# Two transformer layer pairs on one core: the first weight casts before the first turned rows' casts, and the norms' powers before GpSimd's masks

## The chip, the cores and the metric

The kernel runs on one core of one Trainium2 chip. The metric is device microseconds (us) of one execution; a measurement is the median of several runs. Engine names: PE is TensorE (matmuls and transposes), DVE is VectorE, ACT is ScalarE, POOL is GpSimd, SP is SyncE, which here only issues DMAs.

## The reference

Two layers are each applied twice to x of 2048 rows by 640 columns: attention with a window of 256, 32 heads of 20, then a block with a squared ReLU.

```
x = x + A(layernorm(x), wqkv, wo)          # causal, 256 keys back, softmax, times wo
x = x + B(layernorm(x), w1, b1, w2, b2)    # h = relu(x @ w1 + b1) ** 2;  h @ w2 + b2
x = x + A(layernorm(x), wqkv, wo)
x = x + B(layernorm(x), w1, b1, w2, b2)
```

## The kernel before, in words

The rows are cut into 8 groups of 256; with two layers that makes 16 units u. A unit's work is: layer norm; q, k and v (`stage_qk`, `stage_v`); scores, row maxima, exponentials and the product with v, four heads at a time (`max_quad`, `exp_quad`, `pv_quad`); the product with wo (`stage_o`); a second layer norm turned into columns (`stage_y`); and the block B (`stage_f`). Attention of one unit is interleaved with the dense products of the unit before it.

Each large product is done in f16 with both operands split into a high and a low half: three matmuls (high by high, high by low, low by high) stand for one. So each weight piece that arrives in f32 is cast on ACT (high half) and subtracted on DVE (low half): `convert`, lines 270 to 274. Activations that are turned by TensorE get the same pair, a cast on ACT (line 390) and a subtraction on DVE (line 391): `split_t`. The mean and variance of a layer norm come from DVE (lines 366 to 371), the power -0.5 from GpSimd (line 377, a [128,1] op), and DVE then scales the row tile (line 379).

The order on each engine is written out by a planner in the kernel: every piece of work but PE's is posted as a job with an engine, a cost, its dependencies and a priority (`post`). As the planned time passes, `pump` puts the first job of the list that is ready, and a list entry of lower `prio` number stands ahead. The costs and landing times are estimates (`LAND` 1800 ns, `WLAND` 4500 ns after the planned transfer); they decide the order alone. On the chip each engine runs its list in order and waits where an operand is late.

At the start, `ln_load(0, prio=0)` loads the first two row tiles of x and `load_wq` loads wqkv in pieces of 256 or 128 columns, converted 128 columns at a time; `ln_t(0)` turns the first two normed tiles. The masks that GpSimd writes into the exponentials are line 856 (four per four heads; DVE writes two more, line 865).

Of the kernel before, what the change touches and what calls it, by code (L numbers as in the profile page):

```python
# [14 lines left out]
ALU = mybir.AluOpType  # L15

P = 128
# [10 lines left out]
KC = D // P  # L28
# [17 lines left out]
def kernel(ctx: ExitStack, tc: tile.TileContext, x, wqkv, wo, w1, b1, w2, b2, out):  # L46
# [70 lines left out]
    LOOK, LAT, LAND, CROSS, WLAND = 250.0, 50.0, 1800.0, 3600.0, 4500.0  # L117
# [27 lines left out]
    def post(eng, cost, fn, *deps, wait=0.0, prio=1, **kw):  # L145

        j = Job(eng, cost, fn, [d for d in deps if d is not None], now[0] + wait, prio, **kw)
        k = len(pend)
        while k and pend[k - 1].prio > prio:
            k -= 1  # L150
        pend.insert(k, j)
        return j
# [5 lines left out]
    def dma(fn, size, *deps, n=1, cost=450.0, prio=1, **kw):  # L158

        return post("S", n * cost, fn, *deps, prio=prio, size=size, **kw)  # L160
# [109 lines left out]
    def convert(st, hi, low, n, load, *deps, prio=2):  # L270

        a = post("A", 20 + 0.9 * n, lambda: nc.scalar.activation(hi, st, AF.Copy, scale=WS), load, *deps, prio=prio)
        return post("D", 30 + 1.04 * n, lambda: nc.vector.scalar_tensor_tensor(low, st, WS, hi, op0=ALU.mult,
                                                                               op1=ALU.subtract), a, prio=prio)
# [3 lines left out]
    def load_wq():  # L278
        at = 0
        for lo, n in [(j * D + c, min(2 * P, D - c)) for c in (0, 2 * P, 4 * P) for j in range(2)] + [  # L280
                (2 * D + c, min(2 * P, D - c)) for c in (0, 2 * P, 4 * P)]:
            raw, o = (w1raw, at) if at + KC * n <= FC * D else (krow[2], at - FC * D)
            at += KC * n
            st = raw[:, o:o + KC * n].rearrange("p (c n) -> p c n", c=KC)
            load = dma(lambda st=st, lo=lo, n=n:
                       nc.sync.dma_start(st, wqkv[:, lo:lo + n].rearrange("(c p) n -> p c n", p=P)),
                       P * KC * n * 4, prio=0, land=WLAND)
            for z in range(0, n, P):
                c = slice(lo + z, lo + z + P)
                wqj[(lo + z) // P] = convert(st[:, :, z:z + P], wq_s[:, 0, :, c], wq_s[:, 1, :, c], KC * P, load,  # L290
                                             prio=1)

    rowset = {}

# [64 lines left out]
    def layernorm(src, y, *deps, prio=2):  # L359

        box = {}

        def stats(i):
            if i == 0:
                box["st"] = sb.tile([P, 2, 6], F32, name="bst", bufs=2)
            nc.vector.bn_stats(box["st"][:, i, :], src[:, i * HD:(i + 1) * HD])

        def var():
            box["mv"] = mv = sb.tile([P, 4], F32, name="bmv", bufs=2)
            nc.vector.bn_aggr(mv[:, 0:2], box["st"])  # L370
            nc.vector.tensor_scalar(mv[:, 2:3], mv[:, 1:2], 1e-5, YS ** -2, op0=ALU.add, op1=ALU.mult)

        j = None
        for i in range(2):
            j = post("D", 455, lambda i=i: stats(i), j, *(deps[i:i + 1] or deps), prio=prio)
        j = post("D", 400, var, j, prio=prio)
        j = post("G", 520, lambda: nc.gpsimd.tensor_tensor(box["mv"][:, 3:4], box["mv"][:, 2:3], neghalf,
                                                                   op=ALU.pow), j, prio=prio)
        j = post("D", 576, lambda: nc.vector.tensor_scalar(y, src, box["mv"][:, 0:1], box["mv"][:, 3:4],
                                                           op0=ALU.subtract, op1=ALU.mult), j, prio=prio)  # L380
        return j
# [43 lines left out]
    def ln_load(u, *deps, prio=2):  # L425

        l, g = divmod(u, NG)
        ys = []
        for i in range(2):
            xt = sb.tile([P, D], F32, name="xt", tag="xt", bufs=2)  # L430
            load = dma(lambda xt=xt, i=i: nc.sync.dma_start(xt, xsrc(l, 2 * g + i)), P * D * 4, *deps, prio=min(prio, 1))
            ys.append((xt, layernorm(xt, xt, load, prio=prio)))
        lns[u] = ys
# [608 lines left out]
    def stage_o(u):  # L1042
        if u not in ols:
            yield Want(opened, bank=False)
        od, x1b, js, xj = ols.pop(u)
        for i in range(2):
            x1, adds = x1b[i], []
            yield Want(*js[2 * i:2 * i + 2])
            need(*js[2 * i:2 * i + 2])
            for h in range(2):  # L1050
                yield Want()
                acc, jobs = mm_tile([P, 2 * T], "acc")
                hs = slice(h * HD, (h + 1) * HD)
                need(*woj.values())
                def add(x1=x1, acc=acc, hs=hs):
                    nc.vector.scalar_tensor_tensor(x1[:, hs], acc[:, :HD], 1.0 / (OS * WS), x1[:, hs],
                                                   op0=ALU.mult, op1=ALU.add)

                yield from mm3(acc[:, :HD], lambda a, k: od[:, k, a, i * P:(i + 1) * P],
                               lambda c, k: wo_s[:, c, k, hs], KC, 136,  # L1060
                               lambda wait: jobs.append(post("D", 408, add, xj[i], wait=wait, prio=0)))
                adds.append(jobs[0])
            y = sb.tile([P, D], F32, name="xt", tag="xt", bufs=2)
            x1s[u, i], ys[u, i] = x1, (y, layernorm(x1, y, *adds, prio=urgency["ln"]))
# [267 lines left out]
    spin(14)  # L1332
    ln_load(0, prio=0)
    load_wq()
    run(ln_t(0))
    spin(7)
# [91 lines left out]
```

## Time and profile before

| what | value |
|---|---|
| median of 3 runs | 1554.59 us (1553.53 to 1555.71) |
| the profiled execution's own time | 1555.59 us |
| its span in the trace | 1553.9 us |
| PE busy | 1530.8 us, 99% of the span |
| DVE / ACT / POOL busy | 67% / 43% / 29% |

The span runs from the first to the last record of the trace; the time has another 1.7 us around it. The profiled execution took 1.0 us more than the median. All stretches below are counted in us from the span's start. A row of the timeline gives start, duration (from the first start to the last end where several are merged), engine, line and operation, the tile written and the tile read, how many, and in brackets the idle time before it and what ended that.

### The profile page before, as it was taken

To read this page: it belongs to the slowest core of one execution; us is meant where nothing else is said; L and a number is where in the kernel's file an instruction comes from. 1 tells how busy PE (TensorE), PEld (TensorE's weight loads), DVE (VectorE), ACT (ScalarE), POOL (GpSimd) and SP (SyncE) were. 2 spreads that over 40 slices of the span, in tenths; PEclk is the share of its full clock that TensorE was granted. 3 is DMA by queue.
4 is the path that set the end of the run, shared out by engine and by line. 5 is a ranking of instruction groups with operands and counts; after the bars stand their busy time and mean duration, and the time that the engine had idled before them with its cause. 6 is when DMAs were issued, how large, how long until landed. Compare 5 with 4: busy or idle time off the path is not lost.

```text
span 1553.9 us, 58533 instructions
## 1 busy us (share of the span) xinstructions
PE 1530.8 (99%) x25832; PEld 1197.5 (77%) x25832; DVE 1036.8 (67%) x2246; ACT 670.0 (43%) x1367; POOL 453.0 (29%) x847
## 2 busy tenths in 40 slices
PE   8998999999999999999999999999999999999999
PEld 7766778787787877778777787877878777786777
DVE  8788775666766567665656767667665676767641
ACT  4564445344443534534343443444435345354422
POOL 1223314133231322314132241332314224142321
PEclk9999999999999999999999999999999999999999
DMA  9773353442534334343353434435343352432010
GB/s 283 206 224 100 78 130 86 117 101 80 127 69 125 86 105 114 61 128 79 110 130 65 122 82 130 89 81 128 67 131 79 104 121 62 121 86 64 27 62 18
DMA packets 240343, 162.34 MB, mean 104 GB/s; under 512 B 93016, under 2 KB 224088, under 8 KB 240088
## 3 DMA queue, kind: packets, MB, share of 16 engines
q1 hardware_dynamic: 234136, 149.09, 38.0%
q10 hardware_dynamic: 5952, 9.50, 2.1%
q8 instruction: 203, 3.33, 0.9%
q14 instruction: 52, 0.43, 0.1%
HBM read 79.76 MB, written 58.72 MB: 89 GB/s over the span
## 4 chain that ended last, share of the span: by engine, by line
PE 94%; DVE 3%; ACT 1%; issue 1%; POOL 0%; ACTq 0%; DVEq 0%; POOLq 0%
PE acc L340 74%; PE pv L933 8%; PE bb L705 5%; PE bb L842 5%; PE bb L933 2%; ACT pt L827 1%; DVE mx L722 1%; DVE bb L685 0%; PE bb L737 0%; PE bb L888 0%; DVE bb L719 0%; DVE qd L538 0%; POOL pt L856 0%; PE tr L404 0%; DVE mx L685 0%
## 5 line engine op out<-in xcount | busy, mean ns | idle before, releaser
L827 ACT ACTIVATE pt<-bb 128x640 f32<-128x640 f32 (+2 forms) x512 | 312.5, 683 | 164.7 <-PE bb L842 141.0
L856 POOL TENSOR_SCALAR_AFFINE_SELECT pt<-pt 64x256 f32<-64x256 f32 x448 | 198.5, 443 | 595.9 <-ACT pt L827 566.7
L340 PE MATMUL acc<-y,w_s 128*128 128x256 f16 x2880 | 330.3, 273 | 2.3 <-DVE y L391 2.1
L340 PE MATMUL acc<-w_s,hh 128*128 128x320 f16 (+1 forms) x2340 | 326.7, 297 | 0.1
L340 PEld LDWEIGHTS <-w_s 128*128 128x128 f16 x2880 | 276.2, 98 | 42.1 <-issue 3.2
L340 PEld LDWEIGHTS <-hh 128*128 128x128 f16 x2340 | 222.1, 98 | 86.8 <-issue 0.4
L722 DVE TENSOR_REDUCE mx<-bb 128x4 f32<-128x1024 f32 x224 | 273.1, 1223 | 6.7
L340 PE MATMUL acc<-yT,wq_s 128*128 128x256 f16 x2250 | 259.0, 273 | 2.4 <-DVE mT L797 0.7
L340 PEld LDWEIGHTS <-wq_s 128*128 128x128 f16 x2400 | 229.6, 98 | 36.5 <-issue 3.4
L865 DVE COPY_PREDICATED_SCALAR pt<-drop,zero 128x256 f32 x224 | 99.8, 498 | 138.9 <-ACT pt L827 138.6
L1121 POOL TENSOR_TENSOR r<-r 128x256 f32<-128x256 f32 x192 | 122.6, 659 | 214.6 <-ACT r L1117 212.0
L945 ACT COPY ot<-pv 128x256 f32<-128x256 f32 x128 | 47.7, 372 | 287.5 <-PE bb L933 255.3
L933 PE MATMUL pv<-pt,vt 64*32 64x128 f32 (+5 forms) x3840 | 168.1, 303 | 0.9 <-ACT vt L624 0.9
L1127 DVE TENSOR_TENSOR hh<-r,hh 128x256 f16<-128x256 f32 x192 | 90.5, 484 | 108.7 <-ACT hh L1124 104.3
L933 PE MATMUL bb<-pt,vt 64*32 64x192 f32 (+3 forms) x3584 | 154.6, 302 | 0.4 <-POOL pt L856 0.4
L719 DVE COPY_PREDICATED bb<-maskq,bb 128x256 f32<-128x256 uint16 x224 | 94.0, 424 | 84.8 <-PE bb L705 84.1
L933 PEld LDWEIGHTS pv<-pt,vt 64*32 64x32 f32 (+1 forms) x3840 | 126.1, 106 | 31.5 <-issue 3.3
L340 PE MATMUL acc<-wo_s,od 128*128 128x320 f16 x960 | 139.6, 300 | 2.1 <-ACT od L1024 2.0
L340 PE MATMUL acc<-wq_s,yT 128*128 128x320 f16 x900 | 130.4, 299 | 1.6 <-DVE kt L391 0.5
L1117 ACT ACTIVATE r<-acc,b1s 128x256 f32<-128x256 f32 x192 | 81.2, 477 | 95.3 <-PE acc L340 93.4
L340 PEld LDWEIGHTS <-od 128*128 128x128 f16 x960 | 91.1, 98 | 40.4 <-ACT od L1024 2.3
L933 PEld LDWEIGHTS bb<-pt,vt 64*32 64x32 f32 x3584 | 116.3, 106 | 1.6 <-POOL pt L856 0.9
(105 smaller groups left out, 1444.8 us busy)
## 6 DMA issues: line engine op xcount, KB each, us to landing
o<-ot SPq DMA_DIRECT2D x64, 256.0 KB
qt<-qk SPq DMA_DIRECT2D x30, 480.0 KB
kt<-qk SPq DMA_DIRECT2D x30, 480.0 KB
qk<-qd SPq DMA_DIRECT2D x15, 640.0 KB
od<-o SPq DMA_DIRECT2D x14, 640.0 KB
qk<-yl SPq DMA_DIRECT2D x13, 640.0 KB
xt<-in_A_x_dram SPq DMA_DIRECT2D x16, 320.0 KB
x<-in_A_x_dram SPq DMA_DIRECT2D x16, 320.0 KB
```

The costliest lines, as they stand in the source:

```text
L340: nc.tensor.matmul(acc, lhs(a, c), rhs(b, c), start=(k == 0), stop=(k == 3 * nk - 1))
L705: nc.tensor.matmul(flat[e][rows, o:o + b - a], qt[r, p, i * P + 64 * h:i * P + 64 * (h + 1)], kt[r, p, a + to:b + to], start=True, stop=Tr ...
L719: nc.vector.copy_predicated(wins[:, :, 4 * Q:], later, wins[:, :, :Q])
L722: nc.vector.tensor_reduce(most, wins[:, :, Q:], axis=mybir.AxisListType.X, op=ALU.max)
L827: return lambda: nc.scalar.activation(room_of(box)[:, a:b], bank[:, a:b], AF.Exp, scale=SCALE / (QS * QS))
L842: nc.tensor.matmul(flat[e][h * Q:(h + 1) * Q, c0:c1], kt[r, 2 * qd + j, k0:k0 + Q], qt[r, 2 * qd + j, q:q + c1 - c0], start=True, stop=Tru ...
L856: nc.gpsimd.affine_select(out=m, in_=m, pattern=[[0, 4], [-1 if k else 1, Q]], base=0, fill=0.0, compare_op=ALU.is_gt if k else ALU.is_ge, ...
L865: nc.vector.copy_predicated(m, drop[:, k:k + 1, :].bitcast(mybir.dt.uint16).to_broadcast([P, 4, Q]), zero.unsqueeze(1).to_broadcast([P, 4, ...
L933: nc.tensor.matmul(pv[h][32 * jj:32 * (jj + 1), q0 * Q:(q0 + w) * Q], vf[r, c:c + 32], boxes[e]["pt"][r, a:b], start=(k == 0), stop=(k == ...
L1117: nc.scalar.activation(box["r"], acc[:, f, :], AF.Relu, bias=b1s[:, f0 + f:f0 + f + 1], scale=1.0 / (YS * WS))
L1121: nc.gpsimd.tensor_tensor(box["r"], box["r"], box["r"], op=ALU.mult)
L1127: nc.vector.tensor_sub(hh[:, 1, f, :], box["r"], hh[:, 0, f, :])
```

## The change

Three arguments change. The planner is told that the first piece of wqkv lands sooner (`LAND` in place of `WLAND`); the cast and the subtraction of that piece's first 128 columns get priority 0 in place of 1; and the power of every layer norm gets priority 0 in place of the norm's own.

```
-                       P * KC * n * 4, prio=0, land=WLAND)
+                       P * KC * n * 4, prio=0, land=WLAND if at > KC * 2 * P else LAND)
...
                 wqj[(lo + z) // P] = convert(st[:, :, z:z + P], wq_s[:, 0, :, c], wq_s[:, 1, :, c], KC * P, load,
-                                             prio=1)
+                                             prio=0 if lo + z < P else 1)
...
         j = post("G", 520, lambda: nc.gpsimd.tensor_tensor(box["mv"][:, 3:4], box["mv"][:, 2:3], neghalf,
-                                                                   op=ALU.pow), j, prio=prio)
+                                                                   op=ALU.pow), j, prio=0)
```

What the planner makes of it. On ACT, at the start of the program (the first two rows below are the branch into the kernel and the load of the activation table; wq_s are the converted weights, w_s the place where the raw piece lands, yT the turned rows, bb the PSUM banks that hold the transposes):

```order
 L1423 UNCONDITIONAL_BRANCH
-L390 ACT_TABLE_LOAD
+L272 ACT_TABLE_LOAD
+L272 ACTIVATE wq_s<-w_s 128x5x128 x2
 L390 CAST yT<-bb_143 128x3x128
 L390 CAST yT<-bb_143 128x2x128
 L390 CAST yT<-bb_144 128x3x128
 L390 CAST yT<-bb_144 128x2x128
-L272 ACTIVATE wq_s<-w_s 128x5x128 x6
+L272 ACTIVATE wq_s<-w_s 128x5x128 x3
```

Both casts of the first piece (256 columns, two casts) moved from behind the four casts of the turned rows to ahead of them. On DVE one subtraction of the piece (line 273) moved the same way, ahead of the four of line 391; the second stays behind them.

On GpSimd, at the second layer norm of unit 0 (`stage_y`, around 130 us): pt holds the exponentials, bmv the statistics of a norm.

```order
 L377 TENSOR_TENSOR bmv<-bmv,neghalf 128x1
-L856 AFFINE_SELECT pt<-pt 64x4x64 x4
-L377 TENSOR_TENSOR bmv<-bmv,neghalf 128x1
+L856 AFFINE_SELECT pt<-pt 64x4x64
+L377 TENSOR_TENSOR bmv<-bmv,neghalf 128x1
+L856 AFFINE_SELECT pt<-pt 64x4x64 x3
 L1073 TENSOR_TENSOR x_1540<-x_1540,b2s 128x320 x2
```

The power of the second row tile moved ahead of three of the four masks. On DVE at the same place (line 379 scales that row tile, line 391 is the low half of the turned y, lines 719 and 722 find the row maxima in the banks, line 948 adds up the attention's output):

```order
 L273 SCALAR_TENSOR_TENSOR w_s<-kt_97,w_s 128x640
+L379 TENSOR_SCALAR xt<-x_1541,bmv 128x640
 L865 COPY_PREDICATED pt<-drop,zero 128x4x64 x2
 L719 COPY_PREDICATED bb_143<-maskq,bb_143 128x4x64
 L273 SCALAR_TENSOR_TENSOR w_s<-kt_97,w_s 128x640
-L379 TENSOR_SCALAR xt<-x_1541,bmv 128x640
-L722 TENSOR_REDUCE mx<-bb_143 128x4
 L391 TENSOR_TENSOR y_2056<-tr,y_2056 128x3x128
 L391 TENSOR_TENSOR y_2056<-tr,y_2056 128x2x128
```

The scaling moved ahead of two masks, a merge and a weight subtraction, and the maxima of the first bank moved behind the low halves. On PE the five transposes of that tile moved from behind the product with v (line 933) to ahead of it; on ACT the casts of the turned y moved ahead of the copy of that product (line 945).

Elsewhere: on PE four matmuls of the first v product moved from behind the first score matmuls (line 737) to ahead of them, and on ACT the first load of wo is issued one cast later. In most of the later units GpSimd's order "four masks, power, power" became "two masks, power, two masks, power", with no other engine's order changed there. In unit 1 the second norm's scaling moved up on DVE, and with it a turning DMA (line 460) on SP ahead of a store and of the turn of the maxima (line 779).

## Rows read from the trace of the kernel before

**Rows 1.** The page: busy us, share of the span and instructions of each engine.

```profile
PE 1530.8 (99%) x25832; PEld 1197.5 (77%) x25832; DVE 1036.8 (67%) x2246; ACT 670.0 (43%) x1367; POOL 453.0 (29%) x847
```

**Rows 2.** Stretches: busy us by engine, PE clock granted, DMA share, GB/s.

```profile
120.00:160.00 40.00, 34.65 (x629) 27.00 (x632) 32.82 (x64) 20.77 (x42) 16.55 (x27) 0.96 0.32 92
200.00:400.00 200.00, 200.00 (x3628) 157.75 (x3627) 136.01 (x272) 85.55 (x174) 56.48 (x104) 1.00 0.41 102
```

**Rows 3.** Timeline of the start, all engines.

```profile
4.14 1.22 DVE L366 BATCH_NORM_STATS2 bst<-xt 128x6 f32<-128x320 f32 x3
7.86 0.48 ACT L390 CAST yT<-bb 128x384 f16<-128x384 f32 x1 [5.77 <-PE bb L404]
8.37 0.56 DVE L391 TENSOR_TENSOR yT<-bb,yT 128x384 f16<-128x384 f32 x1 [0.31 <-ACT yT L390]
8.96 1.03 ACT L390 CAST yT<-bb 128x256 f16<-128x256 f32 x3 [0.62 <-DVE yT L391]
9.87 3.89 ACT L272 ACTIVATE wq_s<-w_s 128x640 f16<-128x640 f32 x6
10.03 0.89 DVE L391 TENSOR_TENSOR yT<-bb,yT 128x384 f16<-128x384 f32 x2 [0.23 <-ACT yT L390]
10.83 1.55 DVE L273 SCALAR_TENSOR_TENSOR wq_s<-w_s,wq_s 128x640 f16<-128x640 f32 x2
11.70 16.33 PE L340 MATMUL acc<-yT,wq_s 128*128 128x256 f16 x148 [0.63 <-DVE wq_s L273]
```

**Rows 4.** Stretches of the start; columns as in rows 2.

```profile
1.50:4.03 2.53, 2.53 (x12) 2.53 (x13) 2.33 (x13) 0.59 (x1) 2.34 (x8) 1.00 0.79 257
1.50:6.33 4.83, 4.83 (x28) 4.81 (x28) 4.52 (x22) 0.59 (x1) 3.23 (x10) 1.00 0.86 271
```

**Rows 5.** Timeline around the first score matmuls.

```profile
27.87 3.29 PE L340 MATMUL acc<-wq_s,yT 128*128 128x320 f16 x23
31.63 0.30 DVE L685 CUSTOM_DVE_ANT_0 bb<-bb,maskw 128x128 f32<-128x128 f32 x1 [0.18 <-PE bb L737]
```

**Rows 6.** Timeline of unit 0's second norm, all engines.

```profile
132.00 0.15 DVE L371 TENSOR_SCALAR bmv<-bmv 128x1 f32<-128x1 f32 x1
132.13 2.93 POOL L856 TENSOR_SCALAR_AFFINE_SELECT pt<-pt 64x256 f32<-64x256 f32 x4 [5.24 <-ACT pt L827]
132.80 0.88 DVE L865 COPY_PREDICATED_SCALAR pt<-drop,zero 128x256 f32 x2
133.58 0.43 DVE L719 COPY_PREDICATED bb<-maskq,bb 128x256 f32<-128x256 uint16 x1
135.15 0.55 POOL L377 TENSOR_TENSOR bmv<-bmv,neghalf 128x1 f32<-128x1 f32 x1
135.73 1.14 DVE L379 TENSOR_SCALAR xt<-x,bmv 128x640 f32<-128x640 f32 x1 [0.95 <-POOL bmv L377]
137.02 0.74 PE L404 MATMUL tr<-ident,xt 128*128 128x128 f32 x5 [1.24 <-DVE xt L379]
138.70 4.24 PE L340 MATMUL acc<-y,w_s 128*128 128x256 f16 x25 [0.94 <-DVE y L391]
```

**Rows 7.** A stretch of it (columns as in rows 2); 25 like matmuls later.

```profile
140.00:141.00 1.00, 1.00 (x6) 0.67 (x5) 1.00 (x2) 0.00 (x0) 0.00 (x0) 0.50 0.00 0
160.98 2.90 PE L340 MATMUL acc<-y,w_s 128*128 128x256 f16 x25
```

**Rows 8.** Timeline of a later unit, GpSimd, DVE and PE.

```profile
268.20 0.15 DVE L371 TENSOR_SCALAR bmv<-bmv 128x1 f32<-128x1 f32 x1
268.34 1.85 POOL L856 TENSOR_SCALAR_AFFINE_SELECT pt<-pt 64x256 f32<-64x256 f32 x4 [2.11 <-ACT pt L827]
270.96 0.60 DVE L379 TENSOR_SCALAR xt<-xt,bmv 128x640 f32<-128x640 f32 x1
273.08 0.40 PE L933 MATMUL pv<-pt,vt 64*32 64x256 f32 x1
...
274.38 1.80 PE L340 MATMUL acc<-w_s,hh 128*128 128x320 f16 x12
```

## Prediction

> **What bounds the kernel now.** I read the page's busy times first: PE is busy for 99% of the span, every other engine for two thirds or less [rows 1]. So only a stretch in which PE waits can give or lose time. The stretches say where those are: from 200 to 400 us PE has no idle time at all, while from 120 to 160 us it is busy for 34.65 of 40 us and its granted clock averages 0.96 [rows 2]. The other place that the change touches is the start, where the long run of matmuls begins at 11.70 us, on a weight subtraction of DVE [rows 3]. The timelines of these two places carry the sum.
>
> **The first piece of weights.** Before, ACT sat idle for 5.77 us ahead of the first cast of the turned rows at 7.86, and the piece's casts came behind those, from 9.87. DVE's subtraction of the piece came last, at 10.83, and the matmuls ran on when it was done, at 11.70 [rows 3]. Now the casts stand first, and all hangs on when the piece lands. No row shows it; the bounds are these. The x tiles are 655 kB, the first piece is as much again. Up to 4.03 us 2.53 us at 257 GB/s moved 650 kB, that is x; up to 6.33 us 4.83 at 271 moved 1309 kB, that is x and the piece [rows 4]. So it lands no sooner than 6.33. DVE took up the second x tile, the third of its three statistics from 4.14 on, by 4.95 without idling [rows 3], at most 0.92 us behind x's last byte; with the same lag the piece lands by 7.25. The other ceiling is 9.87, where ACT took it up without a wait [rows 3]. I take 6.8, the middle of the near bounds.
>
> From 6.8, two casts at 0.65 (3.89 us for six [rows 3]) let the turned rows' first cast start at 8.1 and end at 8.6. DVE is free at 8.06 (8.37 less its idle 0.31), and its subtraction of the piece takes 0.8 [rows 3]: the first subtraction of turned rows starts at 8.86 in place of 8.37. From there the chain is the old one, 2.55 us to the end of the fourth (10.92 [rows 3]), now 11.41. The second matmul waits for that; the matmuls run on from it, which before they did from the third at 11.70. One matmul is 0.11 us (16.33 for 148 [rows 3]), so the gain is 11.70 - 11.45 - 0.11 = **0.14 us**. It is nothing if the piece lands at 7.2: then the first turned cast ends at 9.0, and the whole saving is spent. Bounds: -0.14 at 6.33 too, since DVE is then the one that decides, and +2.7 at 9.87 (first subtraction at 11.68).
>
> **Four matmuls ahead of the first scores.** They are 3.29/23 = 0.143 us each, 0.57 in all, and push the first scores back. DVE waited for those scores (0.18 us idle ahead of the first maximum) [rows 5], and its maxima are the next thing that PE waits for. So I charge 0.57 - 0.14 = **+0.43 us**, start included; the bounds are -0.14 (the maxima do not bind) and +0.57. The wo load that is issued one ACT cast later has the whole first attention ahead of its use, and I cost it at nothing; without that cover it would cost at most the time that the issue moves, 0.57 us and one cast.
>
> **The power at the second norm, the term that matters.** The statistics were ready at 132.15; GpSimd was in four masks from 132.13 to 135.06; the power followed at 135.15, the scaling at 135.73, the transposes at 137.02, and the matmuls on y resumed at 138.70 [rows 6]. The idle time of 1.24 and 0.94 us ahead of the last two is PE's. Now one mask stands ahead of the power. Four masks took 2.93 us here and 1.85 in a later unit [rows 6, 8]; if all the excess is in the first, it ends at 133.2 (else near 132.6). Taking 133.2: the power ends at 133.8. The scaling is 0.60 or 1.14 [rows 8, 6], so it ends at 134.4 to 134.95, and the transposes go out then. Behind it on DVE stand two masks (0.8), the merge (0.35), a weight subtraction (0.75) and the first low half (0.56) [rows 3, 6]: done at 136.9 to 137.4, and the matmuls on y resume at 137.0 to 137.5. That is 1.2 to 1.7 us sooner; I take **-1.45**.
>
> What moved behind: the product with v now waits for DVE's masks, which stand behind the scaling (135.3 to 135.8), and for the last three of GpSimd's, about 135.8 by the same clock. It takes 1.30 us (273.08 to 274.38 [rows 8]) and so ends near 137.1, about when the low half does: hidden, by nothing to spare. The first bank's maxima, now behind the low halves, are due before the scores that need the banks; 25 matmuls (2.90 us [rows 7]) lie between, so I cost them at nothing; if that cover is too short, PE waits for the rest at those scores.
>
> **The clock.** The 25 matmuls from 138.70 took 4.24 us, like ones 2.90 [rows 6, 7]; the granted clock at 140 us is 0.50, that is 1.2 in place of 2.4 GHz [rows 7]. PE had idled around a 0.74 us burst of transposes just before [rows 6]. That pair of gaps is what the change closes, so I take the clock to stay up: **-1.34**; the other bound is 0.
>
> **The other powers: nothing.** In the later units the statistics are ready at 268.35, the masks run from 268.34; after two of them (269.3) the power goes at once. The last two masks end 0.55 later, at 270.75, and the product with v starts at 273.08 [rows 8]: 2.3 us of cover. The scaling waits at 270.96 behind DVE's own masks in either order. PE has no idle time there to give [rows 2]. The turning DMA that SP issues ahead of the maxima in unit 1 falls into stretches without PE idle, too.
>
> **The sum.** 1555.59 (the profiled time; its span is 1553.9) + 0.43 - 1.45 - 1.34 = 1553.23. The profiled run lies 1.0 us above the median, and 1.34 for a clock that may fall in one run and not in another is of that size. If every run lost it, the median becomes 1552.2, if the median run did not, 1553.6; I take half of the 1.0 us off: **1552.7 us**.
>
> **Rivals.**
> The clock falls all the same. For it: PE's wait for the exponentials ahead of all this stays as it is. Against it: the second pair of gaps, right ahead of the slow matmuls, goes. 1555.59 + 0.43 - 1.45 = 1554.6, for the median **1554.0**.
>
> The gain is eaten between GpSimd and DVE: the power lets DVE's scaling and masks run beside the three masks left over. For it: masks that take 0.46 us alone averaged 0.73 here, and the scaling took 1.14 in place of 0.60 when GpSimd was at work [rows 6, 8]. Against it: two DVE masks ran beside GpSimd's at 0.88 and were not slowed [rows 6]. If all three masks' 1.4 us falls on DVE's chain, y is ready at 138.4 to 138.8 and the clock falls as before: 1555.59 + 0.43 - 0.1 = 1555.9, for the median **1555.3**. It decides from 1.4 us on. The Trainium skill's GPSIMD Engine Reference (section 8, Key points) says that GpSimd shares its SBUF interfaces with VectorE and contends with instructions in a two-port mode or with two SBUF inputs. By that rule the scaling and the weight subtraction would be the ones that contend, which the trace's 1.14 bears out.
>
> The other side: the piece lands late, and the four casts of the turned rows queue behind a waiting cast, with DVE's subtractions behind them and the matmuls last. It decides from 7.2 on, and costs more than all the gains together only near the ceiling of 9.87: +2.7 and +0.57 against -1.45 and -1.34 gives 1556.1, for the median **1555.5**, slower by 0.9. For it: further weight pieces stand in the queue behind the first. Against it: x's lag of at most 0.92 [rows 3, 4]. The Trainium skill's DMA: Bandwidth & Descriptors (section Anatomy of one DMA) gives a fixed cost of some 2 us, most of it the receipt behind the last byte, for DMAs that GpSimd issues. By that the piece would land near 8.3, the start would lose about 1.1 us, and the sum would be 1554; x's lag in the trace is under half of it.
>
> **How the numbers follow.** Forecast 0.45; clock falls 0.25; eaten 0.13; late piece 0.10; something else 0.07, of either sign. The range is 1551.2 (both the turn's better bound and no charge for the four matmuls) to 1555.4, where the two lesser rivals lie. Within 0.2% is about what a measurement of this kernel can tell from no change, 3.1 us here, so faster means below 1551.5 and slower above 1557.7. All four cases lie between; only tails reach out: the forecast's better bounds together with a run-to-run difference of 1 us as between the runs of before (0.14), and a late piece that also disturbs later waits (0.06).
>
> **What would show it.** The piece's first cast starts between 6.4 and 7.25, and the long run of matmuls by 11.7; a start of the cast beyond 7.2 with a later run shows the late piece. The first maximum of DVE starts near 32.06. At the second norm the power starts near 133.2, the transposes near 134.7, the matmuls on y near 137.3, with a granted clock of 1.00 up to 142; a scaling of over 1.1 us and masks near 0.7 show the eaten gain. From 160 on every time is earlier by one and the same amount; a difference that grows there would make the prediction wrong, as would a product with v that ends well after 137.4.

## The result

The changed kernel takes 1560.97 us (median of 6 runs, 1559.13 to 1563.17), the kernel before beside it 1555.34 (6 runs, 1553.53 to 1558.28). The ratio is 1.0035, with a 95% interval of 1.0022 to 1.0048: slower by 5.6 us. The forecast was 1552.7, the range 1551.2 to 1555.4: outside, on the other side. The profiled execution took 1560.78 us with a span of 1559.1, 5.2 us more than that of before. One run of the kernel before in the last batch below took 2196.46 us at a granted clock of 0.653; medians and ratios leave it out.

The timeline of the start after the change, all engines, answers to [rows 3, 5]:

```profile
9.09 1.36 ACT L272 ACTIVATE wq_s<-w_s 128x640 f16<-128x640 f32 x2 [7.00 <-DMA w_s<-in_A_wqkv_dram]
10.85 0.56 DVE L391 TENSOR_TENSOR yT<-bb,yT 128x384 f16<-128x384 f32 x1 [0.17 <-ACT yT L390]
13.12 18.29 PE L340 MATMUL acc<-yT,wq_s 128*128 128x256 f16 x149 [0.60 <-DVE yT L391]
35.01 0.50 PE L737 MATMUL bb<-kt,qt 60*128 60x128 f16 x8
37.01 0.43 ACTq L301 DMA_DIRECT2D w_s<-in_A_wo_dram  x1
37.55 0.75 ACT L390 CAST kt<-tr 128x384 f16<-128x384 f32 x2 [1.05 <-DVE mx L685]
38.67 0.77 PE L404 MATMUL tr<-ident,xt 128*128 128x128 f32 x5 [1.68 <-DVE kt L391]
40.38 4.42 PE L340 MATMUL acc<-wq_s,yT 128*128 128x320 f16 x19 [0.49 <-DVE kt L391]
```

The timeline of the same place in the kernel before, ScalarE and TensorE:

```profile
30.89 0.39 ACTq L301 DMA_DIRECT2D w_s<-in_A_wo_dram  x1
31.09 0.50 PE L737 MATMUL bb<-kt,qt 60*128 60x128 f16 x8
33.02 0.47 ACT L390 CAST kt<-tr 128x384 f16<-128x384 f32 x1
34.34 0.77 PE L404 MATMUL tr<-ident,xt 128*128 128x128 f32 x5 [0.73 <-DVE kt L391]
36.05 2.74 PE L340 MATMUL acc<-wq_s,yT 128*128 128x320 f16 x19 [0.49 <-DVE kt L391]
```

Stretches after the change, TensorE alone (busy us, granted clock, DMA share, GB/s):

```profile
13.00:16.00 3.00, 2.88 (x14) 0.53 0.91 258
40.00:44.00 4.00, 3.62 (x15) 0.57 0.93 294
139.00:146.00 7.00, 4.28 (x88) 0.54 0.44 133
```

The first cast waited 7.00 us for its piece, which was there at 9.09, not at 6.8. The run of matmuls began at 13.12 (before 11.70, with one matmul less in it: 1.53 later). TensorE had idled for 1.53 and 0.60 us just ahead; the granted clock fell, to a mean of 0.53 from 13 to 16 us, and 149 matmuls took 18.29 us, 1.85 more than 149 at the rate of before. The first scores are 3.92 late, and so far that is 1.53 + 1.85 + 0.54 for the four matmuls. Then something new: the casts of line 390 wait 1.05 us longer, the transposes behind them 1.68 in place of 0.73, the clock falls a second time (0.57 from 40 to 44 us), and the 19 matmuls take 4.42 in place of 2.74. (The view puts the casts' wait down to VectorE's maxima; e11 below, with VectorE's order unchanged, has no such wait.) ScalarE's eviction of the product with v (line 945) is a good landmark. Its rows in the timeline before the change:

```profile
51.52 0.37 ACT L945 COPY ot<-pv 128x256 f32<-128x256 f32 x1 [0.44 <-PE pv L933]
150.71 0.37 ACT L945 COPY ot<-pv 128x256 f32<-128x256 f32 x1
```

And the same two after it:

```profile
57.41 0.37 ACT L945 COPY ot<-pv 128x256 f32<-128x256 f32 x1 [0.43 <-PE pv L933]
156.58 0.37 ACT L945 COPY ot<-pv 128x256 f32<-128x256 f32 x1
```

It is 5.89 late at 57 us and 5.87 at 157: the start lost it all, and the second norm, which was to give 2.79 (turn and clock), gave nothing. The timeline of that place after the change answers to [rows 6]; take 5.75 off for the clock of before (its statistics are ready at 137.75, before at 132.00):

```profile
137.88 1.02 POOL L856 TENSOR_SCALAR_AFFINE_SELECT pt<-pt 64x256 f32<-64x256 f32 x1 [5.24 <-ACT pt L827]
138.88 0.54 POOL L377 TENSOR_TENSOR bmv<-bmv,neghalf 128x1 f32<-128x1 f32 x1
139.45 0.80 DVE L379 TENSOR_SCALAR xt<-x,bmv 128x640 f32<-128x640 f32 x1 [0.82 <-POOL bmv L377]
140.17 0.87 DVE L865 COPY_PREDICATED_SCALAR pt<-drop,zero 128x256 f32 x2
140.40 1.30 PE L404 MATMUL tr<-ident,xt 128*128 128x128 f32 x5 [1.19 <-DVE xt L379]
141.28 1.33 DVE L273 SCALAR_TENSOR_TENSOR w_s<-kt,w_s 128x640 f16<-128x640 f32 x1
142.54 0.88 DVE L391 TENSOR_TENSOR y<-tr,y 128x384 f16<-128x384 f32 x2
143.23 0.60 PE L933 MATMUL pv<-pt,vt 64*32 64x256 f32 x1 [1.54 <-DVE y L391]
145.55 3.26 PE L340 MATMUL acc<-y,w_s 128*128 128x256 f16 x25
```

The power and the transposes come when the prediction said (133.13 and 134.65 by the old clock). But the product with v now stands behind the transposes and starts only when the first low half is done, at 143.23; before, it filled the wait for the power. Its bank comes from the same two buffers that both transposes have just taken (`mm_tile`, lines 402 and 914), so it needs a low half to free one. It runs at half clock to 145.55, and the matmuls on y start 1.1 us later than before by the old clock. Their 25 take 3.26 in place of 4.24, and the balance is +0.12. From 160 us on the same copy stays 5.5 to 6.05 us late up to 1434 us. There TensorE waits 1.97 us in both traces, and the clock falls behind that wait in the trace of before alone. The row and the stretch of before:

```profile
1434.69 1.24 PE L340 MATMUL acc<-wo_s,od 128*128 128x320 f16 x4 [1.97 <-ACT od L1024]
1432.00:1440.00 8.00, 5.95 (x133) 0.79 0.09 30
```

And those of after:

```profile
1440.74 0.97 PE L340 MATMUL acc<-wo_s,od 128*128 128x320 f16 x4 [1.97 <-ACT od L1024]
1438.00:1446.00 8.00, 5.95 (x147) 1.00 0.09 30
```

So the 0.7 us between 5.87 and the 5.2 of the end is a fall of the clock that one traced run had and the other had not, and no gain of the later powers.

### The profile page after: what moved, and what is told of

Read it like the earlier page. It is cut to its first block, busy times and chain, and to the rows that moved or that the text cites. A ratio compares the mean times of both kernels' runs of the same rounds, so it can differ in the third digit from the quotient of the medians.

```text
span 1559.1 us, 58546 instructions
## 1 busy us (share of the span) xinstructions
PE 1534.2 (98%) x25832; PEld 1199.8 (77%) x25832; DVE 1036.2 (66%) x2246; ACT 670.1 (43%) x1367; POOL 450.4 (29%) x847
```

## The experiments

Theory: the start lost the 5.6 us and the powers give nothing. First rival: the powers lost it, through GpSimd and VectorE standing in each other's way. Each experiment starts from the kernel named in its diff; the median of before beside it was 1555.72, 1555.74, 1554.45 and 1555.95 us in the four batches.

**The two halves of the change.**

```diff
 e1_powers, from before
-  op=ALU.pow), j, prio=prio)
+  op=ALU.pow), j, prio=0)
 e2_casts, from before
-  P * KC * n * 4, prio=0, land=WLAND)
+  P * KC * n * 4, prio=0, land=WLAND if at > KC * 2 * P else LAND)
-  prio=1)
+  prio=0 if lo + z < P else 1)
```

e1_powers, expected: 

> The norms' powers alone stand ahead of the masks; the first piece's casts stay where they were. Theory (the start lost it, the powers give nothing): in the trace after the change the product with v waits 1.5 us for the low half of the very transposes that now stand ahead of it, so the early power is spent, and the clock falls to 0.50 before the transposes as it did. The time is within 1 us of the kernel before, 1554 to 1556; the power at the second norm starts near 133.2, the product with v only near 137.4, the matmuls on y near 139.8. Rival (the powers lost it, through GpSimd and VectorE standing in each other's way in all units): 1558 or more, with every later unit a little longer. Rival (the powers do gain the 2.8 us forecast and the start alone hides it): 1552.5.

e2_casts, expected: 

> The first piece's casts alone stand ahead of the turned rows' casts; the powers stay behind the masks. Theory (the start lost it): the copy of the last low half into the output of the first group comes 5.9 us later than before, as in the trace after the change, and nothing gives it back: 1561.0, from 1560 to 1562. The first cast starts near 9.1, the matmuls' run near 13.1, the granted clock falls to 0.50 from 13.4 for 3 us and from 40.4 for 3 us. Rival (the powers lost it): within 2 us of the kernel before, below 1557.5.

The powers alone: 1556.74 us, ratio 1.0006 (0.9997 to 1.0015). The casts alone: 1559.38, ratio 1.0028 (1.0017 to 1.0038), single runs from 1555.8 to 1562.6. The first rival falls; the casts carry the loss, and the two ratios add up to that of the whole change. The powers alone come out 1.0 us longer, above the 1554 to 1556 that was expected, and their interval holds both no loss and 2 us. In their one trace 1.0 us of that is lost at 122.75 us: the copy of line 945 stands on ScalarE behind two issues of weight loads that went out late (ScalarE in e1's timeline).

```profile
121.34 1.37 ACTq L325 DMA_DIRECT2D kt<-in_B_w_dram  x2
122.75 0.37 ACT L945 COPY ot<-pv 128x256 f32<-128x256 f32 x1 [3.53 <-DVE x L1056]
```

In the trace of the casts alone the piece was there at 8.29, the clock stayed up at 13 us, and the copy at 51.5 is 3.32 late. The loss differs from run to run, which the theory had not said: 1560 to 1562 was expected.

**The clock at the start.**

```diff
 e4_filled, from after
-    spin(7)
+    spin(15)
```

Expected: 

> The changed kernel with 15 in place of 7 idle matmuls behind the first transposes, so that TensorE is busy until about 12.7 us, through the wait for the late piece. Theory (of the 5.9 us that the start lost, 1.85 is the clock that falls after TensorE stood idle from 10.7 to 13.1): the run of 149 matmuls starts near 13.1 as after the change but takes 16.4 us in place of 18.3, and the whole is 1.9 us shorter than the changed kernel, 1559.1; the second fall, at 40.4, is its own and stays. If the second fall hangs on the first, 3.5 us shorter, 1557.4. Rival (the matmuls of the start are slow for another reason, the transfers of weights or the subtractions beside them): no change against the changed kernel, 1561, the run still 18.3 us.

Measured 1560.52, ratio 1.0033 (1.0021 to 1.0045). In its trace the clock is 1.00 from 13 to 20 us, and the matmuls of the start take 0.11 us each, as before, though the piece came at 8.87 (TensorE in e4's timeline):

```profile
12.89 14.79 PE L340 MATMUL acc<-yT,wq_s 128*128 128x256 f16 x134 [0.55 <-DVE yT L391]
27.95 1.80 PE L340 MATMUL acc<-yT,wq_s 128*128 128x256 f16 x15 [0.26 <-DVE stg L538]
```

So the slow matmuls of the start are the clock's, and the rival's transfers and subtractions are not it. The copy at 51.5 is 4.18 late in place of 5.89. The second fall stays (transposes after 1.75 us of waiting, the 19 matmuls 4.42). But the time hardly fell, against the 1559.1 expected: this trace lost 1.0 us again from 58 to 79, and 1.6 at 120, where TensorE waited 1.44 us for its own issue ahead of line 842. Whether all its runs lose that is open.

**What makes the second wait: the four matmuls, or the load of wo?**

```diff
 e6_chunk_ahead, from before
             todo.pop(0)
             if kind == "m":
+                if n == 0:
+                    c = next(dense)
+                    used[0] += c
+                    step(c)
 e7_filled_sooner, from e4_filled
-  if not all(... and j.end <= now[0] + LOOK for j in wants):
+  ahead_by = 600.0 if (kind, n) == ("m", 0) else LOOK
+  if not all(... and j.end <= now[0] + ahead_by for j in wants):
 e11_wo_elsewhere, from after
-  nc.scalar.dma_start(raw[:, c0:c0 + n], v[:, c0:c0 + n])
+  (nc.gpsimd if c0 == 0 else nc.scalar).dma_start(raw[:, c0:c0 + n], v[:, c0:c0 + n])
```

e6_chunk_ahead, expected: 

> The kernel before with nothing but the four matmuls of the first v product put ahead of the first scores, as the change puts them. Theory (taking these four out of the stretch behind the first scores leaves TensorE idle there long enough for the clock to fall): the first scores come 0.55 us later, the wait ahead of the last transposes of the start grows from 0.73 to 1.7 or 1.8 us, the clock falls to 0.50 and the 19 matmuls behind take 4 us in place of 2.74; the copy at 51.5 us comes 2.3 us later and the whole is 2.3 us longer, near 1558. Rival (the clock falls there only because the start was late, as the prediction's charge of 0.57 us would have it): 0.4 to 0.6 us longer, 1556.2, the 19 matmuls at 2.74 us.

e7_filled_sooner, expected: 

> The changed kernel with 15 idle matmuls in place of 7, and with the first scores let through 0.35 us sooner in the planner's own time, which puts the four matmuls back behind them. Theory: what is left of the start's loss is the late piece alone, 1.5 us; the copy at 51.5 us comes 1.5 us later than before in place of 5.9, with no clock fall before 130 us; with the 0 to 1 us of the powers the whole is 1556.5 to 1558. Rival (the losses of the start do not add up this way; the time comes back as other waits, as with the idle matmuls alone): 1559 or more.

e11_wo_elsewhere, expected: 

> The changed kernel with one transfer moved: the first load of wo is issued by GpSimd in place of ScalarE; every other instruction keeps its place, the four matmuls ahead of the first scores too. Theory (ScalarE held the casts of the turned rows behind that issue, which waited for an earlier transfer): the casts start right behind the eviction of v, 1.0 to 1.6 us sooner than after the change, the wait ahead of the last transposes of the start is back at 0.7 to 0.9 us, the 19 matmuls behind them take 2.74 us, and the whole is 2 to 2.6 us shorter than the changed kernel: 1558 to 1559, or 1557 where the piece lands early enough to keep the clock at the start. Rival (the four matmuls that are missing there as cover make that wait): still 1.6 us and a clock of 0.50 behind it, 1560 to 1561.

e6 measured 1563.73, ratio 1.0053 (1.0039 to 1.0066), and tells little: the planner's times moved with the four matmuls, and it ordered the work from 57 us on anew, where the trace loses some 6.5 us. At the start, which it was made for, the 19 matmuls took 2.75 and the copy is 0.39 late: the rival's side.

e7 measured 1558.13, ratio 1.0015 (1.0006 to 1.0024), 2.4 us under e4, from which it differs in the place of the four matmuls and of the load of wo. Its traced run is the shortest of its eleven, 1555.30 us. It had the piece at 6.69, and there the copy is 0.81 late, with no fall of the clock before 130. The 0.81 is no price of the piece: the matmuls began at 12.11, when the idle matmuls ended.

e11 measured 1559.05, ratio 1.0018 (1.0009 to 1.0027), where the changed kernel has 1.0035. Its timeline, ScalarE and TensorE:

```profile
35.77 0.44 ACT L624 ACTIVATE vt<-acc 128x320 f32<-128x320 f32 x1 [2.15 <-PE acc L340]
36.10 0.47 ACT L390 CAST kt<-tr 128x384 f16<-128x384 f32 x1
37.97 0.77 PE L404 MATMUL tr<-ident,xt 128*128 128x128 f32 x5 [1.27 <-DVE kt L391]
39.67 2.74 PE L340 MATMUL acc<-wq_s,yT 128*128 128x320 f16 x19 [0.49 <-DVE kt L391]
```

With the four matmuls still ahead, but the issue off ScalarE, the casts follow the eviction at once, the transposes start 3.26 us behind the first scores (34.71) as they did before (34.34 - 31.09 = 3.25; after the change 3.66), and the clock stays up. The wait of 1.27 is longer than 0.73 only because four matmuls of work no longer fill it. So the second loss, 0.41 of wait and 1.68 of clock, is the load's issue on ScalarE; by the ratios the time fell by 2.6 us, where 2 to 2.6 was expected, though the two intervals overlap. In ScalarE's list of the changed kernel the issue waits for the semaphore of an earlier transfer, with the casts behind it:

```
L624 ACTIVATE vt_98<-acc 128x16x20 [waits PE_49] x2
L301 DMA w_s<-in_A_wo_dram 128x1280 [waits DMAHW5_49]
L390 CAST kt_97<-tr 128x3x128 [waits DVE_49,PE_49]
```

In the trace after the change it went out at 37.01, 0.5 us behind the eviction that ended at 36.50. The packed trace also keeps the sixteen signals by which each of these transfers reports, as updates of its semaphore. The semaphore that the issue waits for is the one that it raises itself; SyncE's store of line 584 had used it last. Fifteen of that store's signals were in by 36.54, the sixteenth came at 36.99, and the issue went out 0.02 us later. So it was in six traces with this order (after, both repeats, e2, e4 and e9), 0.42 to 1.14 us behind the eviction. The two late issues of e1 followed such a last signal, too (at 121.27 and 122.28).

**When the piece lands.**

```diff
 e8_alone, from after
-  P * KC * n * 4, prio=0, land=...
+  P * KC * n * 4, *([wqj[0]] if wqj else []), prio=0, land=...
 e3_half_piece, from after
-  for lo, n in [(j * D + c, min(2 * P, D - c)) for c in (0, 2 * P, 4 * P) for j in range(2)] + [
+  for lo, n in [(0, P), (P, P), (D, 2 * P)] + [(j * D + c, ...) for c in (2 * P, 4 * P) for j in range(2)] + [
-  land=WLAND if at > KC * 2 * P else LAND
+  land=WLAND if at > KC * 2 * P else 2700.0
 e9_own_queue, from after
-  nc.sync.dma_start(st, wqkv[:, lo:lo + n]...)
+  (nc.scalar if lo == 0 else nc.sync).dma_start(st, wqkv[:, lo:lo + n]...)
```

e8_alone, expected: 

> The changed kernel, with every later piece of the first weights held back until the first piece has been cast, so that this piece has the queue to itself behind x. Only the start of its first cast is of interest (7.0 us of waiting, to 9.09 us, after the change). If the piece lands late because the transfers behind it take turns with it on the 16 engines: the cast starts between 6.4 and 7.3, as the prediction had it from bytes alone. If it lands late for a cost that every transfer has, however much is queued behind: still at 8.5 to 9.1. The time as a whole is longer, since the later pieces come late.

e3_half_piece, expected: 

> The changed kernel with the first piece of 256 columns loaded as two of 128, each cast when it is there. Only the start of the first cast is of interest. If the transfers queued behind take turns with the piece: half the bytes are through in half the time, the first cast starts between 7.3 and 8.2. If it is a cost per transfer: within 0.4 us of 9.1. The scaling of the second row tile stands behind the first half's subtraction here, so the time as a whole says nothing.

after_again, expected: 

> The changed kernel once more, unchanged, for the landing alone: in the runs so far the first cast of the first piece started at 9.09, 8.29, 8.87 and 8.89 us, and at 6.69 in one. If the landing differs from run to run, the cast starts somewhere between 6.5 and 9.2 here, and 0.18 us ahead of it SyncE's issue of the fifth piece ends, as in those; the time follows it. If it is fixed for a kernel: 9.0 to 9.2 again.

after_again2, expected: 

> The changed kernel a third time, for the landing alone, with the same two answers: anywhere between 6.5 and 9.2 if it differs from run to run, 9.0 to 9.2 if it is fixed for a kernel.

e9_own_queue, expected: 

> The changed kernel with one transfer moved: the first piece of weights is issued by ScalarE, at about 1 us, in place of SyncE behind x; every other instruction keeps its place. Theory (the late landing makes the run of matmuls late and lets the clock fall at the start; the four matmuls cost the second fall by themselves): the first cast starts by 7.0, the run of matmuls by 11.6, without a clock fall at 13 us, while the wait ahead of the last transposes of the start stays near 1.75 us with the clock at 0.50 behind it: 2.3 us at the start, and 0 to 1 for the powers, 1557.5 to 1559. Rival (x comes late by as much, the two share the 16 engines): x's statistics end later than 6.3, the run starts at 12 or later and the time stays at 1560 or more.

e8 (1571.45 us, one run) did not do what it was for: the dependency moved the later loads in the planner's time only, on the chip they went out as before (361 GB/s from 7 to 9 us). Its cast started at 8.89, one more landing. e3: 6.47, sooner than either answer had it, with the whole at 1555.09 us in its one run. The changed kernel itself again: 8.30 and 8.43, with 1559.4 and 1558.86 us and the copy 4.20 and 3.58 late. So the landing differs from run to run, and the time goes with it. In each of these traces SyncE's fifth weight issue ends 0.18 to 0.21 us ahead of that first cast. SyncE's row of that issue in the timeline after the change:

```profile
5.12 3.79 SPq L286 DMA_DIRECT2D w_s<-in_A_wqkv_dram  x1
```

In the first repeat:

```profile
5.11 3.01 SPq L286 DMA_DIRECT2D w_s<-in_A_wqkv_dram  x1
```

And in e7:

```profile
4.79 1.72 SPq L286 DMA_DIRECT2D w_s<-in_A_wqkv_dram  x1
```

They end at 8.91, 8.12 and 6.51; the casts start at 9.09, 8.30 and 6.69. The timeline of the kernel before has the same row:

```profile
4.95 3.07 SPq L286 DMA_DIRECT2D w_s<-in_A_wqkv_dram  x1
```

It ends at 8.02: by the same step the piece was there near 8.2 in the run that the prediction argued from. The piece's own signals confirm it, and show what is late (us; read from the packed trace):

| run | 8th signal | 15th | 16th | first cast |
|---|---|---|---|---|
| before | 6.17 | 8.07 | 8.21 | 9.87, did not wait |
| after | 6.25 | 6.97 | 9.07 | 9.09 |
| first repeat | 6.24 | 7.95 | 8.27 | 8.30 |
| second repeat | 6.34 | 8.23 | 8.41 | 8.43 |
| e8 | 6.42 | 7.85 | 8.87 | 8.89 |
| e7 | 6.04 | 6.30 | 6.67 | 6.69 |

Where the cast waited, it starts 0.02 to 0.03 us behind the sixteenth signal. In the 15 traces that load the same 256 columns behind x on SyncE, half the signals are in by 6.04 to 7.12 us, though further pieces are queued behind; the sixteenth comes anywhere from 6.67 to 9.22, and in 14 of the 15 after 7.25. So neither answer of e8 and e3 holds: a cost on the whole transfer, or turns taken with the pieces behind, would hold back the early signals, too. One to several of sixteen parts are late.

e9: 1560.49, ratio 1.0034 (1.0022 to 1.0046). The rival was right. The piece was there by 5.63, but x's second tile came late in turn, and everything with it (ScalarE and VectorE in e9's timeline):

```profile
5.63 1.36 ACT L272 ACTIVATE wq_s<-w_s 128x640 f16<-128x640 f32 x2 [3.05 <-DMA w_s<-in_A_wqkv_dram]
6.43 0.49 DVE L366 BATCH_NORM_STATS2 bst<-xt 128x6 f32<-128x320 f32 x1 [1.47 <-DMA xt<-in_A_x_dram]
```

**The second norm.**

```diff
 e5_turn_later, from e1_powers: transposes of the second tile 1.5 us later in the planner's time
-  yield Want(job, bank=False)
+  yield Want(job, bank=False, soon=[(job, -late_by)] if late_by else ())
 e10_masks_first, from e1_powers: the power of unit 0's second norm counts as ready 1.3 us later
-  self.end = t + TAIL[self.eng]
+  self.end = t + TAIL[self.eng] + self.late
 e12_warm, from e10_masks_first
   for g in between[i:i + 1]:
+      if (u, i) == (0, 0):
+          spin(10)
       yield from g
```

e5_turn_later, expected: 

> The powers alone stand ahead of the masks, and the planner takes up the second norm's transposes 1.5 us later in its own time, which leaves them behind the product with v, as in the kernel before: TensorE's order is that of before throughout. Theory (the product with v, put behind the transposes, is what spent the early power): the product runs near 134.3 as before, the transposes start with its end near 135.9 in place of 137.0, the matmuls on y near 137.6 in place of 138.7, so 1 us shorter than before with the clock falling all the same, 2.4 us with the clock up: 1553 to 1554.5. Rival (an early power gains nothing because GpSimd's masks and VectorE delay each other): as the powers alone, within 0.5 us of it, and the scaling takes 1.1 us again.

e10_masks_first, expected: 

> The powers alone stand ahead of the masks on GpSimd, and at the first unit's second norm the planner counts the power as ready 1.3 us later than it is, so that VectorE's scaling stays behind its masks and TensorE's order is that of the kernel before; only GpSimd's order differs there. Theory (the early power was spent because VectorE then waited for it, 0.82 us, ahead of the masks and the weight subtraction that the product with v and the transposes need): VectorE's masks run at 132.8 as before, the scaling near 134.8 in place of 135.73, the transposes behind the product with v near 135.9, the matmuls on y near 137.5: 1.2 us shorter than the kernel before with the clock falling all the same, 2.5 us with the clock up: 1553.2 to 1554.6. Rival (the masks of GpSimd and VectorE delay each other, and whichever goes first the later is late by as much): no gain, 1555.5 to 1556.5, with the scaling at 1.1 us or the masks near 0.7.

e10_again, expected: 

> The kernel with the powers ahead of the masks and VectorE's scaling kept behind its masks once more, beside the same kernel with idle matmuls. If its 2.2 us in the trace are a gain of every run: 1.5 to 2.5 us below the kernel before on this chip. If its matmuls run at the lower clock in some runs and in some not, as those of the kernel before do: 0 to 1 us below, with single runs 2 to 3 us apart.

e12_warm, expected: 

> The kernel with the powers ahead of the masks and VectorE's scaling kept behind its masks, and with 10 idle matmuls more on TensorE where it waits 2.26 us for the exponentials ahead of the second norm. Theory (in that kernel the clock falls at 133 us after this wait, and slowed the scores and the product with v until 136): the idle matmuls run from 130.5 to 131.8, the granted clock stays at 1.00 up to 140, the product with v ends near 135.3, and the whole is 0.5 to 1 us shorter than without them: 1553.5. Rival (the clock falls there for what TensorE does after that wait, too): no change, or longer where the idle matmuls push the scores back.

e5: 1555.58, ratio 1.0003 (0.9994 to 1.0011); TensorE's order of before is not enough. VectorE still waited 0.82 us for the power with its masks queued behind the scaling, so the product with v, which needs them, ended nearly 2 us later than before.

e10: in its trace the masks run at 132.58, the scaling follows at 135.01 without a wait, and TensorE's rows in the timeline read:

```profile
132.49 1.28 PE L705 MATMUL bb<-kt,qt 60*64 60x256 f16 x37 [0.33 <-ACT pt L827]
136.06 1.08 PE L404 MATMUL tr<-ident,xt 128*128 128x128 f32 x5
137.86 2.89 PE L340 MATMUL acc<-y,w_s 128*128 128x256 f16 x25 [0.72 <-DVE y L391]
```

The transposes wait for nothing, the 25 matmuls run at full clock, and the landmark of 150.71 stands at 148.50, 2.2 us sooner; in the second trace 1.4. The times: 1554.21, ratio 0.9996 (0.9988 to 1.0005), and 1554.27, 0.9989 (0.9980 to 0.9998), the second time, beside e12: 1.7 below before, with single runs 3.2 apart, so less than the traces' gain in every run. Its clock still falls, earlier: 0.57 from 132 to 136, behind the 2.26 us in which TensorE waits for the exponentials.

e12: 1552.16 us (1551.21 to 1552.82, 11 runs), ratio 0.9978 (0.9969 to 0.9987), 2.1 us under e10 beside it, from which it differs in the idle matmuls alone; 0.5 to 1 was expected. They fill that wait. Stretches of e10, columns as above:

```profile
132.00:136.00 4.00, 3.67 (x102) 0.57 0.54 164
136.00:142.00 6.00, 5.19 (x94) 1.00 0.25 66
```

And of e12:

```profile
132.00:136.00 4.00, 3.42 (x91) 1.00 0.56 163
136.00:142.00 6.00, 5.21 (x102) 1.00 0.19 61
```

The clock stays at 1.00, and the runs no longer scatter: 1.6 us from the lowest to the highest, where the 26 runs of before beside them spread over 5.4. This version beats both kernels, before by 0.22%, some 3.4 us. Its traced gain is 1.97 at 150 us, no more than that of e10, and 2.9 at the end. The rest is likely the clock of the runs that were not traced; the mean granted clock of each run points to it. All 11 runs of e12 have 0.999 or 1.000. Of the runs of before beside them, the five at 0.999 average 1553.8 us and the nine at 0.996 average 1557.3.

## Why the prediction was wrong

**"I take 6.8, the middle of the near bounds."** This is the step that failed first. Over nine traced runs in which the first cast could tell, the piece of 256 columns was there at 8.29 to 9.09 in seven (after, e2, e4, e8, e11 and the two repeats), at 6.69 in one; the half piece of e3 at 6.47. The bound of 7.25 came from x's lag behind its bytes. That lag was no guide: by 9.06 us the queue had moved 7.56 us at 311 GB/s, 2351 kB, 1.0 MB more than x and the piece, and the piece had only then been reported. The byte count was right for half of the piece's signals (6.17 in before, against 6.33), but the piece is there with the last of sixteen, which trailed by 0.6 to 3.1 us. The ceiling, 9.87, did hold, and what was the rule in 14 of 15 traces was a rival at 0.10. The trace of before held the answer, in SyncE's fifth issue.

The Trainium skill's DMA: Bandwidth & Descriptors (section Anatomy of one DMA) gives a fixed cost of some 2 us for DMAs that GpSimd issues, and the estimate of 8.3 worked out from it came nearer than the bound from x. But no fixed cost shows in these loads of SyncE's queue: the landings lie 2.5 us apart.

The steps from the landing to the matmuls were right. In e7, with the piece at 6.69, the fourth low half of the turned rows ended at 11.29, where the prediction had 11.41 for 6.8; after the change it ended at 13.40, where the same steps from 9.09 give 13.45 (VectorE, first after the change, then in e7):

```profile
12.51 0.89 DVE L391 TENSOR_TENSOR yT<-bb,yT 128x384 f16<-128x384 f32 x2 [0.23 <-ACT yT L390]
10.40 0.89 DVE L391 TENSOR_TENSOR yT<-bb,yT 128x384 f16<-128x384 f32 x2 [0.23 <-ACT yT L390]
```

**"The other side ... costs more than all the gains together only near the ceiling."** The late piece was priced by its wait alone, +1.1 at 8.3 and +2.7 at 9.87. Wait and clock belong together: a landing at 9.09 cost 1.53 of wait and 1.85 of clock (e4 shows that the second is the clock); at 8.29 to 8.43 the clock stayed up and the run was 0.73 to 0.87 late. The wait alone does not decide: in e8 TensorE idled for 1.61 and 0.60 us at the same place, and the clock stayed at 1.00 from 12 to 16 us. What decides is open.

**"Four matmuls ahead of the first scores": +0.57 at most.** Right as such, 0.54. **"The wo load that is issued one ACT cast later ... I cost it at nothing."** Failed: it is not the load's landing that matters but its issue, which now stands in ScalarE's queue ahead of the casts that TensorE waits for next, and itself waits for the last signal of a store. It cost 0.41 and a fall of the clock, 1.68 (e11). The prediction had asked who needs the load, not who stands behind its issue.

**"The power at the second norm": -1.45.** The power, the scaling and the transposes came at the times given; the step from there failed. The product with v was taken as hidden, "by nothing to spare"; it waited 1.54 us for the low half that frees its bank, and became the bound: it ended near 139.8 by the old clock, against 137.1. e5 and e10 show that the order on VectorE decides: with masks ahead of the scaling the early power is worth 1.4 to 2.2 us in the traces; with the scaling ahead it is worth nothing.

**"The clock": -1.34.** As in the first rival, it fell all the same, to a mean of 0.54 from 139 to 146. In e1 it fell before the product with v. e12 shows, in e10's order, that the wait for the exponentials, which the prediction left as it was, sets it off there.

**The rival on GpSimd and VectorE.** The scaling took 0.80, between the 0.60 and 1.14 of [rows 6, 8], the subtraction behind it 1.33 in place of 0.75: half a microsecond in the middle of the chain, part of the gain that was eaten, and no loss in the later units that the times can tell (the powers alone: 1.0006).

**The range.** Its lower end, 1551.2, does not come out of the two bounds it names: 1552.7 less 0.25 for the turn and 0.57 for the four matmuls is 1551.9. Nothing above hangs on it.

## What to carry to other kernels

An instruction moved ahead in an engine's list takes its wait along: ask of each, transfers' issues included, what can be late for it and who stands behind. Where a row shows only that an operand was there when it was asked for, look for another trace of its arrival, as in the queue that issued it. A transfer is there with the last of its parts; a byte count told here when half of them had come. And a wait of two microseconds on TensorE should be priced with the matmuls behind it at half clock as one of two outcomes, since the same wait had both here; filling one such wait with idle matmuls took 2.1 us off (e12 beside e10).

## What was not expected of the hardware

The landing of one and the same transfer, 655 kB behind 655 kB, lay anywhere from 6.69 to 9.09 us in kernels that issue it alike. The signals show that one to several of its sixteen parts were late. After the change the next two pieces again have one signal well behind the others (8.89 and 10.81; 10.89 and 12.50 us). Why these parts fall behind is open. A load's issue waited for the earlier transfer that had used the same semaphore, and held ScalarE's casts behind it. The weight subtraction of line 273 took 1.33 to 1.35 us beside GpSimd's additions of b2 (e1, e5 and after), 0.81 without. And TensorE's wait of 1.44 us for its own issue, in e4 alone, stays unexplained.
